# Batch 1's keys handed to the DMA queue nine steps ahead of their transposition, where it was four

## The chip, the cores and the metric

The kernel runs on one core of one Trainium2 chip. The metric is the device time of one execution in microseconds (us); lower is better. The engines are PE (TensorE, matrix products), DVE (VectorE), ACT (ScalarE), POOL (GpSimd) and SP (SyncE, which here does nothing but hand transfers to the DMA queue). Each engine works through its own list of instructions in order, and the lists meet only through semaphores.

## The reference, cut to what matters

```python
# q, k, v: (8, 8, 576, 64), p: (8, 8, 32, 64): batch, heads, sequence, width
p_packed = sm_attn(p, k, v)                  # 32 packed rows of each head attend to 576 keys
out = sm_attn(q, p_packed, p_packed)         # 576 queries of each head attend to the 32 packed rows
x = out.transpose(0, 2, 1, 3).reshape(4608, 512)
h = x @ w_in;  x = (h * cos(h)) @ w_out      # first layer, d_ff = 2048
h = x @ w2_in; y = (h * tanh(log1p(exp(h)))) @ w2_out   # second layer
```

The weights are float64 in memory and are turned into float32 on the chip: a load brings a chunk of 128 x 512 doubles (512 KB), ACT and DVE take its high and low words apart and put a float32 together.

## The kernel before, in words

The first layer runs over 4608 tokens in 16 tiles `t` of 288 tokens (two tiles for each batch) and over 16 chunks `s` of 128 hidden features. One pair (t, s) is one **step** n = 16 t + s. At step n PE forms the hidden block `h` in a PSUM bank of a ring of four (`l1`, lines 148 to 150), ACT and DVE make `h * cos(h)` of it (lines 913, 915, 916, 922, 928), and three steps later PE multiplies that with chunk s of `w_out` (`l2`; tile 0 uses line 953, later tiles lines 148 to 150). The last of these, line 928, reads the bank for the last time, so it also sets the bank free. Of tile 0 the chunks of `w_out` are used as plain float32; for the tiles after it ACT casts each to the fast format (line 630) and POOL forms the remainder (line 631).

Everything else is laid beside these steps by a table of step numbers: `at_ld(n, f)` records transfers at step n, `at_pe` and `at_ew` products and element-wise work. The numbers set the order in which the program is recorded; a scheduler then sets the final order on each engine. So one number in the table can move instructions on all five lists.

What stands beside the first steps:

- `w_load` (line 507 loads, lines 520 to 526 convert, 531 stores): the 16 chunks of `w_in`. `w_unit` (line 577) multiplies each with the packed rows of batch 0.
- `wo1_unit` (line 608 loads into one of two buffers `raw`; lines 620, 621 and 625 convert): the 16 chunks of `w_out`, called chunk 0 to 15 here. Chunk n is loaded at step n - 2 and converted at step n. A load can only start when the chunk two before it has been converted.
- `k_unit(b, g)`: the packed rows of batch b, heads 4 g to 4 g + 3. Its loads are eight transfers: four of `p` (line 234, 16 KB each, tile `pc`) and four of `k` (line 153, 272 KB each, tile `kr`, 32 partitions with four runs of 544 floats). DVE transposes both (lines 264 and 159), PE multiplies them (289), DVE takes the maxima (304 to 306), ACT the exponentials (312), PE transposes these (328, 329) and multiplies them with `v` (354; `v` is loaded at lines 244 and 249). There are two buffers `kr`, shared with `q_unit(t)`, which loads the queries of tile t (line 153, four transfers of 272 KB).

For batch 1 the table says `K1_OFF = (13, 18)`: the transposition of heads 0 to 3 is recorded at step 13, that of heads 4 to 7 at step 18, and their loads four steps ahead of it, at steps 9 and 14. The unit of batch 2's heads 0 to 3 and the queries of tile 2 have their loads at step 21.

SP issues transfers in the order of its list. It rotates through eight semaphores, so an issue can also wait for the landing of the transfer that used its semaphore eight transfers earlier.

Of the kernel before, what the change touches and what calls it, by code (L numbers as in the profile page):

```python
# [30 lines left out]
Q_LD = 2  # L31
W_LD = 2
K1_OFF = (13, 18)
K1_LD = 4
W01 = (28, 0.8)
WO_OFF = 0
WO_SPLIT = 13
# [52 lines left out]
def build(tc, q, k, v, p, w1i, w1o, w2i, w2o, out):  # L90
    nc = tc.nc
    ctx = ExitStack()
    with ctx:
# [668 lines left out]
        def after_w(f, lim=CH_LIM):  # L762
            def run():
                if last_w[0] is None or STEP[0] > lim:
                    return f()
                with tc.issue_after(last_w[0]):
                    f()

            return run
# [7 lines left out]
        def at_ld(n, f):  # L777
            bg_ld.setdefault(n, []).append(f)
# [8 lines left out]
        def place(stages, steps, off=0):  # L787
            for (pe, ew), n in zip(stages, steps):
                if off:
                    pe, ew = pe and hp(pe, off), ew and hp(ew, off)  # L790
                if pe is not None:
                    at_pe(n, pe)
                if ew is not None:
                    at_ew(n, ew)
# [11 lines left out]
        for g in range(2):  # L806
            wo = lambda sh: wo_tile(sh, F32)
            wa = lambda sh: wab_tile(0, sh, F32)
            loads, vl, stages = k_unit(0, g, wo)
# [4 lines left out]
        loads, stages = q_unit(0, wa)  # L814
# [19 lines left out]
            at_ew(n + WO_SPLIT, split)  # L834
        for g, off in enumerate(K1_OFF):
            loads, vl, stages = k_unit(1, g, ld_tile)
            at_ld(off - K1_LD, after_w(loads))
            for i in range(3):
                at_ld(off + V_LD + i, after_w(vl[i]))
            place(stages, [off + i for i in K1_SUB])  # L840
# [9 lines left out]
        for j, n in enumerate(U_AT):  # L850
            loads, steps = w2o_unit(j)
# [12 lines left out]
        for pair in range(3):  # L864
# [3 lines left out]
            for b, g, off in zip((b0, b0, b0 + 1, b0 + 1), (0, 1, 0, 1), offs):  # L868
                loads, vl, stages = k_unit(b, g, ld_tile)
# [12 lines left out]
        for t in range(1, NT):  # L882
            n = Q_N[t - 1]
            loads, stages = q_unit(t)
# [438 lines left out]
```

## Time and profile before

| | |
|---|---|
| time, median of 3 runs (lowest to highest) | 1549.7 us (1548.65 to 1550.8) |
| the profiled execution's own time | 1550.71 us |
| its span, first to last instruction | 1548.9 us |
| PE busy | 1479.0 us, 95% |
| DVE busy | 1103.8 us, 71% |
| ACT busy | 888.7 us, 57% |
| POOL busy | 623.8 us, 40% |

Times in the rows further down are microseconds from the start of the span. The page cuts the span into 40 equal slices of 38.7 us; its digits are tenths of busy time, so the stage in question (steps 0 to some 25) is slices 2 to 4. A timeline row gives the start, the time from the first to the last end of a merged group, the engine, the line, the operation, output and inputs, and in square brackets how long the engine sat idle before it and which instruction or transfer ended that.

### The profile page before, as it was taken

What the parts mean: (1) busy time and instruction counts of PE and PEld (TensorE: products, weight loads), DVE (VectorE), ACT (ScalarE), POOL (GpSimd) and SP (SyncE); (2) the same over time, 40 slices, a digit from 0 to 9 for tenths busy, and PEclk for the clock granted to TensorE, in tenths of its full rate; (3) what the DMA queues carried; (4) which work ended last, traced back from release to release, by engine and by line L of the source; (5) the groups of instructions that cost most, each with busy time, mean ns of one, the idle gap of its engine ahead of it and who ended that gap; (6) DMA issues with size and microseconds to landing.
All of it is one profiled execution on the core that took longest, in us unless ns stands there. A gap on an engine that the chain in (4) does not pass through costs nothing.

```text
span 1548.9 us, 28952 instructions
## 1 busy us (share of the span) xinstructions
PE 1479.0 (95%) x9922; PEld 1302.3 (84%) x9922; DVE 1103.8 (71%) x2080; ACT 888.7 (57%) x1834; POOL 623.8 (40%) x618
## 2 busy tenths in 40 slices
PE   7788999999999999999999999999999999999998
PEld 5568778899977999789999887888889898888997
DVE  4786667777677877687775778678668857766756
ACT  3576767667767767666765555334443534454443
POOL 0053333345543654536754666224421622352102
PEclk9899999999999999999999999999999999999999
DMA  7897576445648646623313757668868977876886
GB/s 270 263 259 187 170 184 164 129 111 171 176 132 217 176 139 171 194 89 91 105 51 113 250 212 251 190 201 242 263 214 231 310 216 218 243 213 217 232 263 201
DMA packets 247410, 299.20 MB, mean 193 GB/s; under 512 B 103648, under 2 KB 131040, under 8 KB 247264
## 3 DMA queue, kind: packets, MB, share of 16 engines
q1 hardware_dynamic: 244976, 296.21, 64.1%
q8 instruction: 79, 1.29, 0.4%
q10 hardware_dynamic: 2288, 1.15, 0.3%
q14 instruction: 67, 0.55, 0.1%
HBM read 240.65 MB, written 56.62 MB: 192 GB/s over the span
## 4 chain that ended last, share of the span: by engine, by line
PE 58%; DVE 8%; ACT 5%; DMA 3%; issue 3%; POOL 1%; SPq 1%; DVEq 0%; ACTq 0%; POOLq 0%
PE acc L149 10%; PE acc L150 10%; PE acc L148 10%; PE ps L148 9%; PE ps L149 9%; PE ps L150 9%; DVE r L916 2%; DVE r L915 1%; ACT r L922 1%; DVE r L928 1%; DMA raw<-in_moe_w_out_dram 1%; DVE wab L1020 1%; ACT L922 1%; DMA raw<-in_moe_w_in_dram 1%; PE ps L577 1%
## 5 line engine op out<-in xcount | busy, mean ns | idle before, releaser
L940 POOL TENSOR_TENSOR gh<-r,gh 128x288 fp32r<-128x288 f32 x240 | 199.6, 840 | 302.6 <-ACT gh L937 211.0
L1078 POOL TENSOR_TENSOR gh<-t,gh 128x512 fp32r<-128x512 f32 (+1 forms) x108 | 143.7, 1334 | 352.8 <-ACT gh L1077 343.1
L149 PE MATMUL acc<-gh,wo 128*128 128x288 f32 x960 | 282.5, 299 | 0.6 <-POOL gh L940 0.6
L150 PE MATMUL acc<-gh,wo 128*128 128x288 f32 x960 | 279.2, 297 | 0.0
L148 PE MATMUL acc<-gh,wo 128*128 128x288 f32 x960 | 261.9, 302 | 1.7 <-ACT gh L937 0.9
L149 PE MATMUL acc<-gh,T 128*128 128x512 f32 (+1 forms) x560 | 207.0, 371 | 2.1 <-DVE gh L1078 1.6
L148 PE MATMUL ps<-wab,ws 128*128 128x512 f32 (+1 forms) x560 | 206.0, 369 | 1.6 <-DMA ws<-wst 1.2
L149 PE MATMUL ps<-wab,ws 128*128 128x512 f32 (+1 forms) x560 | 206.4, 369 | 0.0
L150 PE MATMUL ps<-wab,ws 128*128 128x512 f32 (+1 forms) x560 | 205.3, 369 | 0.0
L150 PE MATMUL acc<-gh,T 128*128 128x512 f32 (+1 forms) x560 | 205.1, 369 | 0.0
L148 PE MATMUL ps<-aT,wab 128*128 128x288 f32 x512 | 163.7, 320 | 35.4 <-DVE r L928 21.3
L149 PEld LDWEIGHTS acc<-gh,wo 128*128 128x128 f32 x960 | 182.7, 190 | 6.9 <-issue 5.1
L1078 DVE TENSOR_TENSOR gh<-wo,gh 128x512 fp32r<-128x512 f32 (+1 forms) x160 | 128.0, 806 | 83.3 <-ACT gh L1077 82.8
L922 ACT ACTIVATE r<-r,halfpi 128x288 f32<-128x288 f32 x256 | 135.9, 535 | 88.2 <-DVE r L916 86.0
L148 PEld LDWEIGHTS acc<-gh,wo 128*128 128x128 f32 x960 | 172.5, 190 | 14.8 <-issue 6.1
L150 PEld LDWEIGHTS acc<-gh,wo 128*128 128x128 f32 x960 | 182.2, 190 | 2.1 <-issue 2.1
L148 PE MATMUL acc<-gh,T 128*128 128x512 f32 (+1 forms) x560 | 182.0, 369 | 1.0 <-DMA T<-tst 0.8
L928 DVE TENSOR_TENSOR r<-r,ps 128x288 f32<-128x288 f32 x240 | 107.3, 450 | 72.6 <-ACT r L922 72.3
L913 ACT ACTIVATE ki<-ps,quarter 128x288 int32<-128x288 f32 x256 | 124.6, 497 | 52.8 <-PE ps L150 41.2
L149 PE MATMUL ps<-aT,wab 128*128 128x288 f32 x512 | 154.0, 301 | 0.0
L150 PE MATMUL ps<-aT,wab 128*128 128x288 f32 x512 | 153.7, 300 | 0.0
L148 PEld LDWEIGHTS ps<-aT,wab 128*128 128x128 f32 x512 | 98.7, 193 | 62.2 <-DVE r L928 28.6
(193 smaller groups left out, 3061.7 us busy)
## 6 DMA issues: line engine op xcount, KB each, us to landing
T<-tst SPq DMA_DIRECT2D x280, 256.0 KB, 3.0
ws<-wst SPq DMA_DIRECT2D x224, 256.0 KB, 3.0
ld<-ws SPq DMA_DIRECT2D x80, 256.0 KB, 3.7
kr<-in_q_dram SPq DMA_DIRECT2D x60, 272.0 KB, 5.8
kr<-in_k_dram SPq DMA_DIRECT2D x56, 272.0 KB, 5.3
tst<-wt SPq DMA_DIRECT2D x56, 256.0 KB, 2.1
wst<-ws SPq DMA_DIRECT2D x56, 256.0 KB, 2.7
x2d<-xo SPq DMA_DIRECT2D x64, 144.0 KB, 1.7
```

Source lines behind the costliest of these rows:

```text
L148: nc.tensor.matmul(ps, l0, r0, start=first, stop=False, skip_group_check=more)
L149: nc.tensor.matmul(ps, l0, r1, start=False, stop=False, skip_group_check=more)
L150: nc.tensor.matmul(ps, l1, r0, start=False, stop=last, skip_group_check=more)
L577: return nc.tensor.matmul(st[b][32 * l : 32 * l + 32], PK[(b, g)][r : r + 64, 32 * l : 32 * l + 32], ms[h // 2]["m"][r : r + 64], start=Tr ...
L913: nc.scalar.activation(ki, st["h"], AF.Identity, bias=quarter, scale=1.0 / TWO_PI)
L915: nc.vector.scalar_tensor_tensor(r, ki, -TWO_PI, st["h"], ALU.mult, ALU.add)
L916: (nc.gpsimd if n % C_MOD in C_POOL else nc.vector).tensor_scalar(r, r, 1.570796, -4.712388, ALU.min, ALU.max)
L922: nc.scalar.activation(g, g, AF.Sin, bias=halfpi, scale=1.0)
L928: nc.vector.tensor_tensor(g, r, st["h"], ALU.mult)
L940: nc.gpsimd.tensor_tensor(gh[:, 1], st["g"], gh[:, 0], ALU.subtract)
L1020: (nc.gpsimd if k % 2 == 0 else nc.vector).tensor_tensor(x[:, a, 1, :n], src, x[:, a, 0, :n], ALU.subtract)
L1078: eng.tensor_tensor(hl[:, 1, :n], src, hl[:, 0, :n], ALU.subtract)
```

## The change

One constant becomes a pair, and its use picks an element of it. Both elements are 9, so the loads of batch 1's two key units are recorded at steps 4 and 9 in place of 9 and 14. The transpositions and all that follows them keep their steps.

```diff
-K1_LD = 4
+K1_LD = (9, 9)
...
         for g, off in enumerate(K1_OFF):
             loads, vl, stages = k_unit(1, g, ld_tile)
-            at_ld(off - K1_LD, after_w(loads))
+            at_ld(off - K1_LD[g], after_w(loads))
```

No instruction is added or taken away. What the scheduler makes of it is seen in the lists. The first place is SP's list from the load of chunk 12 on. In the names below `raw` is the buffer of a chunk of `w_out`, `kr` and `pc` hold keys (or queries) and `p`. Before, chunks 12 to 15 stand together, and the keys of batch 1's heads 4 to 7 (`kr_989`) come behind them:

```order
L531 DMA ws_813<-wab_669 128x512
L608 DMA raw_871<-in_moe_w_out_dram 128x1024
L608 DMA raw_898<-in_moe_w_out_dram 128x1024
L608 DMA raw_927<-in_moe_w_out_dram 128x1024
L608 DMA raw_959<-in_moe_w_out_dram 128x1024
L234 DMA pc_988<-in_p_dram 32x4x32
L153 DMA kr_989<-in_k_dram 32x4x544
L234 DMA pc_988<-in_p_dram 32x4x32
L153 DMA kr_989<-in_k_dram 32x4x544
```

Now the last part of that list reads as follows; `raw_937` is chunk 14, `raw_969` chunk 15, `kr_1301` batch 2's heads 0 to 3 and `kr_1310` the queries of tile 2:

```order
L234 DMA pc_1300<-in_p_dram 32x4x32
L153 DMA kr_1301<-in_k_dram 32x4x544
L234 DMA pc_1803<-in_p_dram 32x4x32 x2
L153 DMA kr_1310<-in_q_dram 32x4x544
L608 DMA raw_937<-in_moe_w_out_dram 128x1024
L153 DMA kr_1310<-in_q_dram 32x4x544 x3
L608 DMA raw_969<-in_moe_w_out_dram 128x1024
L244 DMA ld_1040<-in_v_dram 128x2x256
```

Three units (the four transfers each of batch 1's heads 4 to 7, of batch 2's heads 0 to 3 and of tile 2's queries) have moved from behind chunk 15 to ahead of it. Batch 1's heads 0 to 3 stood ahead of chunk 15 already; they have moved from behind chunk 11 to behind chunk 6, ahead of the last four chunks of `w_in`.

The second place is ACT's list from the conversion of chunk 15 (line 620) to the first `r` of tile 1 (`r_1058`, line 922; `ki_1056` is the first step of its chain, line 312 the exponentials of batch 1's heads 0 to 3). Before, chunk 15 stands thirteen rows ahead of the exponentials, and casts, cosines and the chain of tile 0 fill the distance:

```order
L620 ACTIVATE wab_919<-raw_959 128x512
L913 ACTIVATE ki_1023<-ps_998,quarter 128x288
L630 CAST wo_1061<-wo_485 128x512
L630 CAST wo_1097<-wo_486 128x512
L922 ACTIVATE r_977<-r_977,halfpi 128x288
L630 CAST wo_1151<-wo_486 128x512
L630 CAST wo_1207<-wo_487 128x512
L630 CAST wo_1253<-wo_487 128x512
L630 CAST wo_1292<-wo_488 128x512
L630 CAST wo_1351<-wo_488 128x512
L630 CAST wo_1413<-wo_489 128x512
L922 ACTIVATE r_1025<-r_1025,halfpi 128x288
```

Now it is followed by eight casts and the first instruction of two steps of tile 1:

```order
L620 ACTIVATE wab_929<-raw_969 128x512
L630 CAST wo_1061<-wo_485 128x512
L630 CAST wo_1097<-wo_486 128x512
L630 CAST wo_1151<-wo_486 128x512
L630 CAST wo_1207<-wo_487 128x512
L630 CAST wo_1253<-wo_487 128x512
L913 ACTIVATE ki_1056<-ps_1042,quarter 128x288
L630 CAST wo_1292<-wo_488 128x512
L630 CAST wo_1351<-wo_488 128x512
L630 CAST wo_1413<-wo_489 128x512
L913 ACTIVATE ki_1089<-ps_1069,quarter 128x288
L312 ACT_TABLE_LOAD
```

All cosines of tile 0 now stand ahead of chunk 15, and behind it come the casts, `ki` of tile 1's first two steps, a table load, the two exponentials, one more cast, a second table load and the cosine of `r_1058`.

The third place is DVE's list around the transposition of batch 2's heads 0 to 3 (lines 264 and 159, `pc_1300` and `kr_1301`). Now it stands between the maxima of batch 1's heads 0 to 3, with the conversion of chunk 15 (lines 621 and 625) in the middle:

```order
L304 TENSOR_REDUCE sm_1035<-ps_1006 128x1
L304 TENSOR_REDUCE sm_1035<-ps_1005 128x1
L264 STREAM_TRANSPOSE pp_1418<-pc_1300 128x128
L159 STREAM_TRANSPOSE kt_1420<-kr_1301 128x576 x2
L305 TENSOR_REDUCE sm_1035<-sm_1035 128x1
L621 TENSOR_SCALAR cvt_1031<-raw_969 128x512
L306 TENSOR_SCALAR sm_1035<-sm_1035 128x1
```

Before, all four maxima stood together, chunk 15 stood ahead of them, and the transposition came after them, between lines 915 and 916 of `r_1058`.

## Rows read from the trace of the kernel before

**Rows 1.** The page: span, each engine's share, and PE in 40 slices.
```profile
span 1548.9 us, 28952 instructions
PE 1479.0 (95%) x9922; PEld 1302.3 (84%) x9922; DVE 1103.8 (71%) x2080; ACT 888.7 (57%) x1834; POOL 623.8 (40%) x618
...
PE   7788999999999999999999999999999999999998
```
**Rows 2.** Timeline of PE: groups that waited, and three products between them.
```profile
85.27 1.06 PE L577 MATMUL ps<-wab,pk 64*32 64x512 f32 x8 [0.59 <-DVE g L928]
...
117.78 0.40 PE L148 MATMUL ps<-aT,wab 128*128 128x288 f32 x1 [3.74 <-DVE r L928]
...
118.69 0.56 PE L148 MATMUL acc<-gh,wo 128*128 128x288 f32 x3
120.32 0.44 PE L354 MATMUL ps<-ld,a 64*32 64x64 f32 x8 [1.07 <-ACT a L337]
```
**Rows 3.** PE waits from 0 to 300 us: who for whom, total, times, longest.
```profile
PE ps L577 <- DVE wab L526: 1.3, 1, 1.3
```
**Rows 4.** DVE waits from 70 to 150 us, the same columns.
```profile
DVE pp L264 <- DMA pc<-in_p_dram: 1.6, 1, 1.6
...
DVE kt L159 <- DMA kr<-in_k_dram: 0.2, 1, 0.2
```
**Rows 5.** Timeline of DVE ahead of the release at 117.32.
```profile
114.59 0.31 DVE L264 STREAM_TRANSPOSE pp<-pc 128x128 f32<-128x128 f32 x1 [1.63 <-DMA pc<-in_p_dram]
114.82 1.22 DVE L916 TENSOR_SCALAR r<-r 128x288 f32<-128x288 f32 x1
115.97 1.43 DVE L159 STREAM_TRANSPOSE kt<-kr 128x576 f32<-128x576 f32 x2
117.32 0.41 DVE L928 TENSOR_TENSOR r<-r,ps 128x288 f32<-128x288 f32 x1
```
**Rows 6.** Timeline of SP: issues from chunk 12 on; keys and queries behind chunk 15.
```profile
86.79 9.42 SPq L608 DMA_DIRECT2D raw<-in_moe_w_out_dram  x4
96.26 0.42 SPq L234 DMA_DIRECT2D pc<-in_p_dram  x1
...
104.37 0.33 SPq L234 DMA_DIRECT2D pc<-in_p_dram  x1
...
110.01 3.14 SPq L153 DMA_DIRECT2D kr<-in_q_dram  x4
```
**Rows 7.** Stretches: busy time of PE, PEld, DVE, ACT, POOL; clock; DMA share; GB/s.
```profile
82.00:92.00 10.00, 8.79 (x52) 6.06 (x53) 9.83 (x22) 6.75 (x12) 1.46 (x2) 1.00 1.04 295
92.00:98.00 6.00, 3.79 (x20) 2.78 (x19) 6.00 (x12) 5.01 (x10) 4.21 (x3) 1.00 0.49 129
98.00:104.00 6.00, 5.59 (x20) 4.56 (x21) 5.95 (x11) 4.88 (x11) 3.51 (x3) 0.72 1.09 256
104.00:120.00 16.00, 11.51 (x72) 8.77 (x70) 10.81 (x22) 11.75 (x24) 14.35 (x13) 0.98 1.08 243
...
130.00:140.00 10.00, 10.00 (x109) 9.53 (x108) 4.70 (x16) 7.71 (x15) 2.21 (x3) 1.00 0.69 183
140.00:150.00 10.00, 9.23 (x91) 7.86 (x89) 5.71 (x18) 6.55 (x13) 1.61 (x2) 1.00 0.46 128
```
**Rows 8.** DMA from 60 to 82 us, mostly weights: packets, volume, mean rate.
```profile
DMA packets 2582, 7.51 MB, mean 341 GB/s; under 512 B 287, under 2 KB 287, under 8 KB 2581
```
**Rows 9.** Timeline of ACT: chunk 15, casts, the exponentials, and what follows them.
```profile
100.13 0.66 ACT L620 ACTIVATE wab<-raw 128x512 f32<-128x512 f32 x1
...
102.54 3.21 ACT L630 CAST wo<-wo 128x512 fp32r<-128x512 f32 x6
...
109.00 1.28 ACT L312 ACT_TABLE_LOAD   x1 [1.28 <-DVE sm L306]
110.30 0.50 ACT L312 ACTIVATE tmp<-ps,sm 128x288 f32<-128x288 f32 x1
...
111.27 0.50 ACT L913 ACTIVATE ki<-ps,quarter 128x288 int32<-128x288 f32 x1
111.65 0.62 ACT L630 CAST wo<-wab 128x512 fp32r<-128x512 f32 x1
112.29 1.28 ACT L922 ACT_TABLE_LOAD   x1
116.08 0.54 ACT L922 ACTIVATE r<-r,halfpi 128x288 f32<-128x288 f32 x1 [2.51 <-DVE r L916]
...
118.10 0.40 ACT L966 COPY xo<-acc 128x288 f32<-128x288 f32 x1
118.39 0.59 ACT L336 COPY tmp<-ps 128x512 f32<-128x512 f32 x1
...
120.00 0.26 ACT L337 COPY a<-ps 64x128 f32<-64x128 f32 x1
```

## The prediction

> **What bounds the kernel now.** I read the page first, then the stretches of the stage that the change touches, then the timelines of PE, DVE, ACT and SP there. The page says that PE is busy 95% of a span of 1548.9 us and that only the first four of its 40 slices show 7 and 8 tenths [rows 1]. Past some 160 us PE is the bound almost without a gap, so whatever delay it has collected by then stays to the end, and whatever is saved there is kept. The change moves transfers between 60 and 125 us, so the question is when PE gets through that stretch.
>
> In it PE is not its own bound. From 82 to 98 us DVE is busy 9.83 of 10 and 6.00 of 6 us [rows 7]: it converts weights, and PE follows it. From 98 to 120 us the DMA engines are full (share 1.09 and 1.08) [rows 7]. The longest wait of PE in the stretch is one of 3.74 us that ends at 117.78, where a hidden block of tile 1 needs a free PSUM bank, and line 928 on DVE frees it; a second of 1.07 us ends at 120.32 and waits for ACT's copy at line 337 [rows 2]. Behind that PE is busy 10.00 of 10 us from 130 to 140 and 9.23 from 140 to 150 [rows 7]. So **117.78 and 120.32 are the clock by which I judge the change**: if the same two products start later, the kernel ends later by about as much.
>
> What stands ahead of 117.78 in the rows before: DVE waits 1.63 us for the `p` of batch 2's unit, needs 1.22 us for one line 916 and 1.43 us for two transpositions, and only then does line 928 at 117.32 [rows 5]. None of that is batch 1's keys. DVE waited for a key transfer once between 70 and 150 us, for 0.2 us [rows 4]. The change therefore brings early what was hardly waited for; its time comes from what it moves out of the way, or into it.
>
> **The change part by part.** (1) Batch 1's keys themselves. Their arrival saves at most the 0.2 us of [rows 4]; DVE is full there, so the next item is late instead. I take 0.
>
> (2) The first unit now stands ahead of the last four chunks of `w_in`. It is four transfers of 272 KB, 1.11 MB; the DMA engines move 341 GB/s from 60 to 82 us [rows 8] and are full afterwards at 82 to 92 [rows 7]. At the 243 GB/s of a stretch that is mostly keys and queries [rows 7] it costs 1.11 / 0.243 = 4.6 us. By so much the products of line 577 can come later; PE waited 1.3 us for their conversion once already [rows 3]. Whether that reaches 117.78 depends on DVE, which is the fuller engine until 98 us and has the same instructions to do in either order. I take 0, since the unit's bytes lie ahead of chunk 15 in both lists; the cover is DVE's backlog, and without it the cost is up to 4.6 us. That is the upper end.
>
> (3) Chunks 14 and 15 of `w_out` now stand behind the second key unit of batch 1, the first of batch 2 and the queries of tile 2. Before, all four chunks from 12 on were issued between 86.79 and 96.21 and those units followed at 96.26, 104.37 and 110.01 [rows 6]; ACT converted chunk 15 at 100.13 and did not wait for it [rows 9]. Now twelve transfers of 272 KB are queued ahead of it: 3.34 MB. At 243 GB/s that is 13.7 us. Some of it fills a hole: from 92 to 98 us the engines' share was 0.49 [rows 7] because SP stood waiting for a free `raw` buffer, and with keys to move that hole of 6 x 0.51 = 3.1 us closes. So chunk 15 arrives some 10.6 us later, at about 110.7 in place of 100.1. The bounds: 13.7 us without the credit, and 3.34 / 0.341 = 9.8 less 3.1 = 6.7 us if keys went at the rate of [rows 8]. I take the middle one because the 243 GB/s were measured on these very kinds of transfer, at full engines.
>
> (4) What hangs on chunk 15 on ACT. In the new list its conversion (line 620) is followed in order by five casts, a line 913, three casts, another 913, the table load, two exponentials, a cast, the second table load and the cosine of tile 1's first block, then line 928 on DVE. From [rows 9]: 0.6 + 5 x 0.535 (six took 3.21) = 3.3; 913 from 111.27 to 111.65 is 0.4, so 3.7; three casts 1.6, 5.3; 913 0.4, 5.7; table 1.3, 7.0; exponentials from 110.30 to 111.27 1.0, 8.0; cast 0.5, 8.5; table 1.3, 9.8; cosine 0.5, 10.3; line 928 0.4 [rows 5], **10.7 us**. The bank is free at 110.7 + 10.7 = 121.4. Before, the product started at 117.78: **3.6 us later**. DVE's line 306 for the exponentials stands behind chunk 15's line 621 as well, but the two are ready within a microsecond of the arrival and ACT gets to the exponentials 6 us after it, so DVE adds nothing.
>
> The second clock agrees. Line 337 follows the cosine through two copies of line 966, a cast, a second cosine, line 336 and itself: 0.3 + 0.5 + 0.3 + 0.45 + 0.5 + 0.3 = 2.3 [rows 9]. So 110.7 + 10.3 + 2.3 = 123.3 against 120.32, 3.0 later, and three products that lay before line 354 (0.56) [rows 2] now come behind it: 3.5.
>
> (5) What goes. DVE's wait of 1.63 us for batch 2's `p` goes, since that unit now lands ahead of chunk 15, and its transpositions come before the release and not just ahead of it. That would open the bank at 117.32 - 1.63 - 1.43 = 114.3 [rows 5] if ACT were ready. By (4) ACT is not: what is late next is chunk 15. I take 0, and up to 3.1 us plus the second wait of 1.07 [rows 2] is the lower end.
>
> (6) POOL forms the remainders behind ACT's casts and is busy 14.35 of 16 us from 104 to 120 [rows 7]. Its run moves later with the casts. What reads the remainders are the products of tile 1, all behind 117.78, and the casts ahead of the exponentials do not wait for POOL in the row of 102.54 [rows 9]. I take 0.
>
> The sum is 3.5 us. Against the profiled execution's own 1550.71 (span 1548.9 and 1.8 around it) that is 1554.2; the median of the runs is 1.0 below that execution, so 1549.7 + 3.5 = **1553.2 us**. Both are the same shift. A measurement of this kernel can tell some 0.2%, 3.1 us, from no change, so this is just beyond it.
>
> **A rule weighed.** In the rows a stretch of keys and queries moves 243 GB/s at a DMA share of 1.08, and one of weights 341 [rows 7, 8]. The Trainium skill, page "DMA: Bandwidth & Descriptors", section Specifications, gives 512 B as the smallest transfer that runs at line rate. A key run is 544 floats, 2,176 B, so by that rule keys should cost what weights cost, chunk 15 would come 6.7 us later, and the sum would be nothing. The trace disagrees at 243; the measurement decides, and the rule's case is the first rival below.
>
> **The rivals.** *Keys at the weights' rate (no change).* If the keys, spread among other transfers, run at 341 GB/s, chunk 15 lands at 100.1 + 6.7 = 106.8 and the bank opens at 117.5, 0.3 earlier than before: 1549.4. For it: the twelve transfers are now mixed with chunks and stores. Against it: the stretch of 104 to 120 us had up to eight transfers under way as well. Chance 0.20.
>
> *The change does not do what it says (no change).* SP may be held at the new place by its rotating semaphores or by the buffer, so that the keys leave hardly sooner, and chunks 14 and 15 follow as they did. Then the stage keeps its clock: 1549.7. For it: SP stood 9.42 us over four issues [rows 6], so it is often held. Against it: the list has an order, and what is behind a held issue is held too. Chance 0.12.
>
> *The release comes early (faster).* One mechanism: batch 2's `p` and keys are there when DVE reaches them, so the 1.63 us of waiting and the transpositions leave the place ahead of line 928, and ACT follows. It decides in favour if chunk 15 lands before 117.78 - 10.7 = 107.1, and is worth 3.1 us from a landing before 104.0. With the wait for line 337 gone too the gain is 3.1 + 1.07 = 4.2: 1545.5. For it: the 3.74 us of PE are the longest wait in the stretch, and the DMA had a hole. Against it: twelve transfers ahead of chunk 15. Chance 0.21.
>
> **How the numbers follow.** The forecast, slower by the queue ahead of chunk 15, has 0.47, with its own range 1550.5 (landing at 108) to 1558.0 (the 4.6 us of part 2 on top of 3.5, 1557.8). Of that 0.02 falls within 0.2%, so with the rivals' 0.20 and 0.12: faster 0.21, same 0.34, slower 0.45. The range reaches down to the faster rival, a little short of its full gain, and up past part 2 by 1.2 us for a PE that is throttled after a longer wait (from 98 to 104 us, behind a stretch in which PE was busy 3.79 of 6, the clock granted was 0.72, so in part at the lower of its two levels, 1.2 against 2.4 GHz) [rows 7]: 1546.0 to 1559.0.
>
> **What would show it.** Right: in the timeline of ACT after the change the line 620 of chunk 15 starts near 111, after a wait for a transfer of `in_moe_w_out`, and the product that waits for line 928 starts near 121. Part 3 is wrong if chunk 15 lands before 107; part 4 if ACT waits again between it and the exponentials; part 2 if the last products of line 577 (85.27 before [rows 2]) come over 4 us late and the delay is still there at 117. The forecast as a whole is wrong if PE starts that product before 117.8, or if PE, late there, catches up before 160 us.

## The result

The changed kernel takes 1562.07 us in the median of five runs (1559.39 to 1567.32), the kernel before 1549.70 (1544.88 to 1550.80): 12.4 us more by the medians. The recorded ratio is 1.0089, with a 95% interval of 1.0069 to 1.0110. The forecast was 1553.2, slower by 3.5, in a range up to 1559.0. The direction is right, the size is not, and the time lies outside the range.

The profiled execution is the slowest of the five (1567.32, span 1565.5). Its page says that the work is the same, and that the third and fourth of the 40 slices of PE went from 8 tenths to 7, and two later ones from 9 to 8, as against [rows 1]:

```profile
span 1565.5 us, 28952 instructions
...
PE 1482.1 (95%) x9922; PEld 1303.4 (83%) x9922; DVE 1104.2 (71%) x2080; ACT 887.7 (57%) x1834; POOL 621.2 (40%) x618
...
PE   7777999999999989998999999999999999999998
```

The stretches answer to [rows 7], in the same columns:

```profile
82.00:92.00 10.00, 6.05 (x31) 3.67 (x30) 8.23 (x19) 7.47 (x11) 2.36 (x2) 1.00 0.62 219
92.00:98.00 6.00, 5.79 (x36) 3.96 (x34) 5.33 (x11) 3.08 (x6) 1.53 (x2) 1.00 1.10 270
98.00:104.00 6.00, 4.18 (x24) 3.35 (x22) 5.20 (x11) 4.45 (x10) 1.60 (x2) 1.00 1.06 285
104.00:120.00 16.00, 11.94 (x60) 8.68 (x61) 9.12 (x21) 5.68 (x12) 3.97 (x4) 0.89 1.05 257
...
130.00:140.00 10.00, 9.08 (x105) 7.75 (x97) 7.22 (x19) 6.93 (x16) 7.68 (x8) 0.93 0.46 130
140.00:150.00 10.00, 8.67 (x98) 8.33 (x99) 3.75 (x10) 7.35 (x16) 2.37 (x3) 1.00 0.43 91
```

The hole of the DMA engines at 92 to 98 us (share 0.49 before) is filled. But 82 to 92, which had 1.04, now has 0.62: 10 x 0.38 = 3.8 us lost, where 3.1 were lost before. The hole has moved, and PE is down to 6.05 of 10 us in it (8.79 before). ACT and POOL, 11.75 and 14.35 of 16 us at 104 to 120 before, do 5.68 and 3.97: they wait for chunks.

The timeline of SP shows the moved list, where [rows 6] had chunks 12 to 15 in four issues from 86.79 on. The rows are those of chunks 11, 12 with 13, 14 and 15:

```profile
89.43 0.33 SPq L608 DMA_DIRECT2D raw<-in_moe_w_out_dram  x1
...
94.62 0.82 SPq L608 DMA_DIRECT2D raw<-in_moe_w_out_dram  x2
...
104.94 0.35 SPq L608 DMA_DIRECT2D raw<-in_moe_w_out_dram  x1
...
108.62 0.35 SPq L608 DMA_DIRECT2D raw<-in_moe_w_out_dram  x1
```

ACT's timeline answers to [rows 9], from the conversion of chunk 14 on:

```profile
112.56 0.68 ACT L620 ACTIVATE wab<-raw 128x512 f32<-128x512 f32 x1 [4.58 <-DMA raw<-in_moe_w_out_dram]
...
117.03 0.69 ACT L620 ACTIVATE wab<-raw 128x512 f32<-128x512 f32 x1 [3.28 <-DMA raw<-in_moe_w_out_dram]
117.62 2.68 ACT L630 CAST wo<-wo 128x512 fp32r<-128x512 f32 x5
...
120.61 1.64 ACT L630 CAST wo<-wo 128x512 fp32r<-128x512 f32 x3
...
122.66 1.28 ACT L312 ACT_TABLE_LOAD   x1
123.95 0.50 ACT L312 ACTIVATE tmp<-ps,sm 128x288 f32<-128x288 f32 x1
```

ACT waits 4.58 and 3.28 us for the last two chunks, and the exponentials start at 123.95 in place of 110.30. DVE's timeline, for [rows 5], and its waits from 70 to 150 us, for [rows 4]:

```profile
98.43 0.31 DVE L264 STREAM_TRANSPOSE pp<-pc 128x128 f32<-128x128 f32 x1 [1.01 <-DMA pc<-in_p_dram]
...
127.41 0.45 DVE L928 TENSOR_TENSOR r<-r,ps 128x288 f32<-128x288 f32 x1 [1.18 <-ACT r L922]
```

```profile
DVE cvt L621 <- DMA raw<-in_moe_w_out_dram: 4.8, 2, 4.1
...
DVE pp L264 <- DMA pc<-in_p_dram: 1.8, 2, 1.0
```

The 1.63 us for batch 2's `p` are gone, but the waits for `p` sum to 1.8 us as they did to 1.6, and 4.8 us for chunks have come on top. PE, for [rows 2]:

```profile
92.57 1.06 PE L577 MATMUL ps<-wab,pk 64*32 64x512 f32 x8
...
127.92 0.61 PE L148 MATMUL ps<-aT,wab 128*128 128x288 f32 x1 [1.50 <-DVE r L928]
...
129.73 0.44 PE L354 MATMUL ps<-ld,a 64*32 64x64 f32 x8
```

The last products of line 577 come 7.3 us later (85.27 before), the first clock, the product at 127.92, 10.1 later (117.78 before), and the second, line 354, 9.4 later (120.32 before). Set beside each other, the executions of line 928 in the two traces lie 3.4 us apart at 85 us, 10.9 at 160 to 200 and 12.7 at the end of the first layer. This one execution loses up to 4 us more in the second layer; the other four are up to 8 us shorter, and what it loses there was not traced further.

### The profile page after: what moved, and what is told of

Same layout as the page of the kernel before. It is cut to its first block, busy times and chain, and to the rows that moved or that the text cites. A ratio compares the mean times of both kernels' runs of the same rounds, so it can differ in the third digit from the quotient of the medians.

```text
span 1565.5 us, 28952 instructions
## 1 busy us (share of the span) xinstructions
PE 1482.1 (95%) x9922; PEld 1303.4 (83%) x9922; DVE 1104.2 (71%) x2080; ACT 887.7 (57%) x1834; POOL 621.2 (40%) x618
## 4 chain that ended last, share of the span: by engine, by line
PE 53%; DVE 6%; issue 6%; ACT 5%; DMA 4%; POOL 4%; SPq 1%; DVEq 0%; ACTq 0%; POOLq 0%
PE acc L149 10%; PE acc L150 10%; PE acc L148 10%; PE ps L148 8%; PE ps L150 7%; PE ps L149 7%; POOL ws L671 2%; DVE r L916 1%; DMA ws<-wst 1%; ACT r L922 1%; DVE r L915 1%; DMA T<-tst 1%; DVE r L928 1%; DVE wab L1020 1%; PE ps L577 1%
```

## The experiments

`K1_LD` holds how many steps ahead the two units of batch 1 are loaded: (9, 9) in the changed kernel, (4, 4) in the one before. `CH_LIM` is the step from which a load is held behind the last weight chunk. Diffs are against the changed kernel, e17's against the one before. All times in the table are of the profiled execution of each. At 66 us the executions already stand up to 2.5 us from the kernel before, so only larger differences in a column mean something. The last column is the recorded ratio to the runs of the kernel before; microseconds in the text are differences of medians, and the two need not agree exactly (e7: 1.7 us by the medians, 1.0001 by the ratio).

| kernel | chunk 15, L620 | first exponential, L312 | first L354 | ratio (95%) |
|---|---|---|---|---|
| before | 100.13 | 110.30 | 120.32 | 1 |
| changed (9, 9) | 117.03 | 123.95 | 129.73 | 1.0089 (1.0069 to 1.0110) |
| e1 (9, 4) | 104.36 | 120.13 | 127.44 | 1.0081 (1.0061 to 1.0102) |
| e2 (4, 9) | 115.54 | 118.04 | 126.93 | 1.0032 (1.0016 to 1.0048) |
| e3 (9, 9), limit 24 | 109.51 | 116.94 | 128.19 | 1.0042 (1.0028 to 1.0057) |
| e4 (9, 9), casts free | 116.41 | 124.63 | 131.93 | 1.0083 (1.0064 to 1.0101) |
| e5 (4, 9), limit 24 | 107.03 | 113.69 | 118.71 | 1.0041 (1.0026 to 1.0056) |
| e6 (7, 4) | 102.11 | 121.96 | 129.26 | 1.0089 (1.0069 to 1.0109) |
| e7 (4, 7), limit 24 | 101.30 | 108.75 | 117.88 | 1.0001 (0.9990 to 1.0012) |
| e8 (3, 4) | 103.06 | 112.95 | 120.40 | 0.9993 (0.9978 to 1.0007) |
| e9 (9, 9), casts two steps later | 117.19 | 119.69 | 129.44 | 1.0054 (1.0035 to 1.0073) |
| e10 (14, 4) | 103.79 | 115.20 | 124.04 | 1.0032 (1.0018 to 1.0046) |
| e11 (14, 7), limit 24 | 104.33 | 117.98 | 124.64 | 1.0032 (1.0017 to 1.0047) |
| e12 (9, 4), transpositions held | 105.81 | 123.44 | 131.77 | 1.0084 (1.0065 to 1.0103) |
| e13 (14, 4), transpositions held | 99.86 | 112.42 | 119.83 | 0.9984 (0.9968 to 1.0000) |
| e14 (9, 9), transpositions held | 117.84 | 123.98 | 129.78 | 1.0062 (1.0041 to 1.0082) |
| e15 (14, 7), limit 24, held | 100.88 | 119.76 | 127.19 | 1.0053 (1.0037 to 1.0069) |
| e16 (9, 4), casts behind EXP | 104.78 | 114.48 | 123.57 | 1.0041 (1.0024 to 1.0058) |
| e17 (4, 4), casts behind EXP | 103.57 | 113.80 | 122.19 | 1.0016 (1.0004 to 1.0028) |
| e18 e13, casts behind EXP | 102.02 | 112.02 | 120.88 | 1.0002 (0.9990 to 1.0013) |

How much of a loss is there when PE leaves the stage can be counted in the traces. Take PE's products of lines 148 to 150 in order and compare their starts with those of the kernel before. Between 165 and 200 us the changed kernel is 10.9 us behind, e1 10.9, e2 6.9, e3 7.6, e5 0.1, e9 10.4, e12 15.8, e15 7.2, e16 6.4 and e17 4.4; e7 is 2.2 and e13 1.4 ahead. Where this and the ratio part, the loss arises behind the stage.

### Which of the moved loads costs it

```
-K1_LD = (9, 9)
+K1_LD = (9, 4)      # e1: the first unit alone
+K1_LD = (4, 9)      # e2: the second unit alone
-CH_LIM = 20         # e3, e5: batch 2's unit and tile 2's queries
+CH_LIM = 24         #         go back behind chunk 15
```

> Only the first key unit (batch 1, heads 0 to 3) is loaded nine steps ahead; the second is loaded four steps ahead as in the kernel before. Four key transfers (1.09 MB) so pass the last four w_in chunks, and no more data stands ahead of w_out's chunk 15 than in the kernel before. Theory T (the delay is the data queued ahead of chunk 15, some 4.5 us a unit at 243 GB/s, passed on through ScalarE's list): chunk 15 converted between 99 and 104 us (100.1 before, 117.0 in the changed kernel), the product behind the second clock's bank between 117 and 120 us, total +0 to +3 us. Rival R1 (the first unit ahead of the w_in chunks does most of it, by way of VectorE's list of conversions): chunk 15 after 108 us, total +6 to +10 us. Rival R2 (ScalarE's order of casts, pinned behind chunk 15): the order here is that of before, total +0.

> Only the second key unit (batch 1, heads 4 to 7) is loaded nine steps ahead; the first stays four steps ahead. Three units (batch 1 heads 4 to 7, batch 2 heads 0 to 3, query tile 2) then stand ahead of chunk 15 that stood behind it, and ScalarE's list behind chunk 15 is shorter than in the changed kernel (four casts and no cast ahead of the exponentials but one, against eight). Theory T: chunk 15 converted at 111 to 114 us (13.7 us of transfers, with or without 3 us of queue time that stood empty before), the bank's product 6 to 8 us behind it at 118 to 122 us, total +1 to +5 us. R1: 0 to +1 us, chunk 15 at 101 to 104. R2: by the shorter list, total 0 to +1 us wherever chunk 15 lands.

> The changed kernel with batch 2's first key unit and query tile 2 held behind chunk 15 again, as they were in the kernel before; both of batch 1's units stay nine steps ahead. Theory T: one unit more than before stands ahead of chunks 12 to 15, and part of the first unit's detour: chunk 12 as in the changed kernel (100 us), chunk 15 at 105 to 109 us, not 117; ScalarE's list behind it is as long as in the changed kernel, so the bank's product is 10 to 11 us later, 116 to 120 us (127.9 in the changed kernel); total 0 to +3 us. R1 (the first unit does it): total +6 us or more. R2 (the list of casts behind chunk 15, which is longer still here): total +6 us or more.

> The second key unit (batch 1, heads 4 to 7) is loaded nine steps ahead, the first stays at four, and batch 2's first unit and query tile 2 are held behind chunk 15: one unit (1.09 MB), not three, stands ahead of chunks 12 to 15 that stood behind them before. Theory T2 (each unit put ahead of a weight chunk in this stretch delays it by about 4.5 us, and the conversions behind it pass that on through the in-order lists of VectorE and ScalarE): chunk 15 converted at 103 to 106 us (100.1 before), the first unit's exponentials at 113 to 116 us (110.3 before), total +3 to +5 us. Rival S (the delay is made by batch 2's unit and the query tile, which have no slack to use; one unit fits into the 3 us in which the queue stood empty at 92 to 98 us): exponentials within 1 us of before, total -1 to +1 us.

The first unit, which the prediction took at nothing, costs 13.2 us by the medians when it is moved alone, as much as the whole change and more than any of the expectations allowed (e1). The second move costs 6.6 (e2); with two of the three units back behind chunk 15, both units of batch 1 cost 7.6 (e3), and the second of them alone 6.7 (e5). The parts don't add up: 13.2 and 6.6 are more than 12.4, and e3, which moves both units, costs less than e1, which moves one. They delay the same exponentials, and every version has its own lists.

Nor does chunk 15 rank the kernels. In e2 it lands at 115.54, in e1 at 104.36, and e1 is the slower one. So the argument "chunk 15 sets the release" holds for the changed kernel only. ACT's timeline of e1 shows what stands in its place:

```profile
104.36 0.67 ACT L620 ACTIVATE wab<-raw 128x512 f32<-128x512 f32 x1
104.94 4.24 ACT L630 CAST wo<-wo 128x512 fp32r<-128x512 f32 x8
109.08 1.52 ACT L922 ACTIVATE r<-r,halfpi 128x288 f32<-128x288 f32 x3
...
118.83 1.28 ACT L312 ACT_TABLE_LOAD   x1 [5.79 <-DVE sm L306]
```

The scores of line 289 on PE, in the kernel before and in e1, and DVE's timeline of e1:

```profile
105.15 0.72 PE L289 MATMUL ps<-kt,pp 64*32 64x288 f32 x16
```

```profile
111.96 1.21 PE L289 MATMUL ps<-kt,pp 64*32 64x288 f32 x16 [3.34 <-DVE g L928]
```

```profile
106.98 1.76 DVE L625 SCALAR_TENSOR_TENSOR wab<-wab,cvt 128x512 int32<-128x512 int32 x1
108.66 1.37 DVE L916 TENSOR_SCALAR r<-r 128x288 f32<-128x288 f32 x1
109.95 0.30 DVE L264 STREAM_TRANSPOSE pp<-pc 128x128 f32<-128x128 f32 x1
110.18 1.39 DVE L159 STREAM_TRANSPOSE kt<-kr 128x576 f32<-128x576 f32 x2
111.50 1.14 DVE L928 TENSOR_TENSOR g<-r,ps 128x288 f32<-128x288 f32 x3
113.27 0.82 DVE L304 TENSOR_REDUCE sm<-ps 128x1 f32<-128x288 f32 x2 [0.63 <-PE ps L289]
118.22 0.31 DVE L264 STREAM_TRANSPOSE pp<-pc 128x128 f32<-128x128 f32 x1 [4.13 <-DMA pc<-in_p_dram]
...
118.60 0.15 DVE L306 TENSOR_SCALAR sm<-sm 128x1 f32<-128x1 f32 x1
```

Two things delay the exponentials here. The first is the scores: they wait 3.34 us for line 928, which frees their bank, and start at 111.96 (105.15 before). On ACT a block of eight casts stands ahead of three cosines that line 928 needs. But DVE isn't seen waiting for a cosine: its timeline has no gap from 96.18 to 112.64, and between the first of these cosines (done at 109.6) and line 928 its own list has a line 916 and the transposition of batch 1's second unit. How much the casts add is therefore not read from a wait. They add in another way too: they release the remainders on POOL (line 631, nine in a row from 105.61 to 117.31), and beside them lines 625 and 916 take 1.76 and 1.37 us, where e16 has 0.68 and 0.30.

The second comes on top. The maxima are done at 114.09 (108.55 before), but DVE's list has batch 2's `p` ahead of lines 305 and 306, and DVE waits 4.13 us for it. ACT waits 5.79 us for line 306. In the kernel before, this transposition comes behind line 306.

### The hole: filled, or moved

```
-K1_LD = (9, 9)      # e7: the second unit exactly between
+K1_LD = (4, 7)      #     chunks 13 and 14
-CH_LIM = 20
+CH_LIM = 24
```

> The second key unit is loaded seven steps ahead and everything behind it is held behind chunk 15: it stands between chunks 13 and 14, where in the kernel before the queue waits some 7 us for the two raw buffers to come free (its four chunk loads take 9.42 us to hand over, the transfers' share falls to 0.49 at 92 to 98 us). The first unit stays at four. Theory T2 with the hole (transfers that stand where the queue is held anyway cost only what is longer than the hole, 4.5 less 3.1 us): chunk 15 at 100 to 103 us, exponentials at 109 to 112 us, total -2 to +2 us, and batch 2's first unit arrives about 3 us earlier than in the kernel before, so that VectorE's wait of 1.63 us for it is gone. Rival D (any unit ahead of a chunk costs its 4.5 us): chunk 15 at 104 to 106 us, total +3 to +5 us.

e5 and e7 move the same four transfers: in e5 they stand ahead of chunk 12, in e7 between 13 and 14. By the medians the one costs 6.7 us and the other 1.7, by the ratios 1.0041 and 1.0001; e7's interval includes no change. The stretches of e5, then of e7, columns as in [rows 7]:

```profile
92.00:98.00 6.00, 4.94 (x25) 3.96 (x26) 3.65 (x10) 2.62 (x6) 0.67 (x1) 1.00 1.01 260
98.00:104.00 6.00, 2.83 (x10) 1.95 (x9) 6.00 (x13) 3.32 (x7) 2.70 (x2) 0.82 0.45 105
```

```profile
92.00:98.00 6.00, 3.89 (x21) 3.12 (x22) 6.00 (x13) 4.05 (x9) 2.71 (x3) 1.00 1.09 230
98.00:104.00 6.00, 6.00 (x40) 4.21 (x39) 5.93 (x11) 4.82 (x10) 2.86 (x3) 1.00 1.10 331
```

In e5 the hole is as large as before (share 0.45) and stands six microseconds later. Its cause is that chunk 14 goes into the `raw` buffer of chunk 12 and SP waits until DVE and ACT have converted that; SP's timeline of e5 has the same held group as [rows 6], only later:

```profile
91.13 11.16 SPq L608 DMA_DIRECT2D raw<-in_moe_w_out_dram  x4
```

What stands ahead of chunk 12 delays chunk 12, its conversion, and so the hole. What stands right at the wait fills it, as in e7. In this stage the difference is worth 2.3 us (e5 0.1 behind the kernel before at 165 to 200 us, e7 2.2 ahead; at 66 us they stood 0.9 apart). The rest of e5's loss arises behind 250 us: its products are still only 0.3 us late there and 3.9 at the end of the first layer. So the 6.7 us are not the price of the hole.

### The first unit, step by step

```
+K1_LD = (7, 4)      # e6: ahead of fewer chunks
+K1_LD = (3, 4)      # e8: one step later than before
+K1_LD = (14, 4)     # e10: issued at 19 to 30 us, ahead of the last eight w_in chunks
+K1_LD = (14, 7)     # e11, with CH_LIM = 24: e10 and e7 together
```

> The first key unit is loaded seven steps ahead in place of four, the second at four: it passes w_out's chunks 9 to 11 and the last two w_in chunks, but not the two w_in chunks and w_out's chunks 7 and 8 that it passes at nine. Theory T2 (a unit of transfers ahead of a w_in chunk, in a stretch in which the queue never stands empty, delays that chunk's conversion and all behind it, whether VectorE has a backlog or not): the last w_in chunk's product 3 to 6 us later than 85.3 us, total +4 to +8 us. Rival B (VectorE's backlog covers it, as the prediction had it, and the loss in the first-unit-only kernel came from the two chunks at 60 to 72 us, where VectorE waits for data): the product within 1.5 us of before, total -1 to +2 us.

> The other direction: the first key unit is loaded three steps ahead in place of four, between chunk 12 and chunk 13. Theory T2: chunk 12 was not waiting for the unit but for a raw buffer, so it gains little, and the unit arrives 2 to 4 us later than before, with VectorE waiting for it ahead of its transpositions (91.1 us before, with 0.17 us of wait): total +1 to +4 us. Rival E (earlier is only worse, later is better all along): total -1 to -4 us.

> The first key unit is loaded fourteen steps ahead, the second four. The first unit is so handed over at about 18 us, behind the first two w_out chunks, and its transfers fall into the stretch from 28 to 46 us, where the transfers' share is 0.24, 0.45 and 0.22; VectorE's transpositions of it come at 30 and 67 us, when it has no backlog. No w_in or w_out chunk stands behind it that could have been transferred in that time. Theory T2 (what counts is what a unit displaces, not how early it is): no delay of the w_in chunks (products at 82.6 and 85.3 us as before), the unit's 4.5 us of transfers gone from 79 to 92 us and 1.7 us of transpositions gone from VectorE's backlog there, total -5 to 0 us. Rival H (earliness itself costs: the unit holds one of the two key buffers 40 us longer, and the query tile's loads behind it wait for the other): total +2 to +8 us.

> The first key unit fourteen steps ahead, in the stretch where the queue stands empty (28 to 46 us), and the second between chunks 13 and 14 as in the run with the second unit ahead of chunk 14, the rest held behind chunk 15. Theory T2: both units are out of the way of every chunk: chunk 15 at 98 to 102 us, exponentials at 105 to 111 us (110.3 before), total -6 to 0 us, at or a little below the run with the first unit alone in the empty stretch. Rival H (earliness itself costs): +2 to +8 us.

Ahead of fewer chunks the unit costs no less (e6, +15.2 by the medians, where 8 was the most expected); a step later than before it costs nothing (e8). In the emptier queue ahead of 46 us (share 0.25 from 30 to 46 us before) it costs 4.5 (e10), though its bytes should be out of the way there; with e7's move on top it is 5.3 (e11). DVE's and PE's timelines of e10 say why:

```profile
69.10 2.10 DVE L159 STREAM_TRANSPOSE kt<-kr 128x576 f32<-128x576 f32 x3 [0.49 <-DMA raw<-in_moe_w_out_dram]
...
71.69 0.77 DVE L159 STREAM_TRANSPOSE kt<-kr 128x576 f32<-128x576 f32 x1
```

```profile
90.22 1.06 PE L577 MATMUL ps<-wab,pk 64*32 64x512 f32 x8 [0.63 <-DVE g L928]
```

With keys there early, the order of DVE's work changes too: its two transpositions come at 69 to 72 us, next to two of the queries, which the kernel before has at 67.38; they are now ahead of conversions of `w_in`, and the last products of line 577 start at 90.22 in place of 85.27.

### DVE's list

The transpositions of batch 1's first unit are put back behind the conversion of chunk 11; in e12, e13, e14 and e15 with the loads of e1, e10, the changed kernel and e11.

```
 def s0():
-    nc.vector.transpose(pp, ...); st["pp"] = pp; trans(0)
+    with behind(("c", 11) if (b, g) == (1, 0) else None):
+        nc.vector.transpose(pp, ...); st["pp"] = pp; trans(0)
...
-    nc.vector.tensor_scalar(t, st["r"][:, :, 0], 29, ...)
+    marks[("c", ft)] = nc.vector.tensor_scalar(t, st["r"][:, :, 0], 29, ...)
```

> The kernel with only the first unit nine steps ahead, and the unit's transpositions on VectorE held behind the start of chunk 11's conversion, their place in the kernel before. Loads in the order of the first-unit-only kernel (+13.2 us). Theory L (the list: transpositions brought forward, with their waits for the keys, stand ahead of the w_in and w_out conversions): last w_in chunk's product within 2 us of 85.3, total 0 to +5 us. Theory X (the transfers: the chunks come late whatever VectorE's order): last w_in product at 90 to 93 us as without the hold, total +8 to +13 us.

> The first unit loaded in the empty stretch of the queue (fourteen steps ahead) with its transpositions held behind the start of chunk 11's conversion. Against the same loads without the hold (+4.5 us). Theory L: the last w_in product back at 85 to 87 us and the unit's transfers out of the way of chunks 12 to 15, total -3 to +1 us. Theory X (something in the early loads themselves, such as w_in's stores or the key buffer that is held): +3 to +6 us as without the hold.

> The changed kernel (both units nine steps ahead) with the first unit's transpositions held behind the start of chunk 11's conversion. Theory L: the first unit's share goes and the three units ahead of chunk 15 stay, as in the kernel with the second unit alone nine steps ahead (+6.6 us): total +5 to +9 us. Theory X: total +11 to +14 us as in the changed kernel.

> The first unit in the empty stretch with its transpositions held behind the start of chunk 11's conversion, the second unit between chunks 13 and 14, the rest held behind chunk 15. Theory L: total -4 to +1 us, against +5.0 without the hold. Theory X: +3 to +6 us.

In the emptier queue it was DVE's list: e10's +4.5 us becomes -2.9 (e13), and PE's timeline of e13 has the products nearly where they were:

```profile
86.72 1.06 PE L577 MATMUL ps<-wab,pk 64*32 64x512 f32 x8
```

In e1's place it was not: e12 costs 12.6 us where e1 cost 13.2, and its last products of line 577 start at 94.82, no earlier than e1's at 92.69. In the changed kernel it is some 2 of 12.4, if anything (e14, +10.4, the intervals overlap). e15 puts two moves together that cost nothing each, and should have cost nothing; it costs 8.4, though chunk 15 lands at 100.88. ACT's timeline of e15 has the block of eight casts again, and no cosine until 105.60:

```profile
100.88 0.68 ACT L620 ACTIVATE wab<-raw 128x512 f32<-128x512 f32 x1
101.45 4.26 ACT L630 CAST wo<-wo 128x512 fp32r<-128x512 f32 x8
105.60 0.55 ACT L922 ACTIVATE r<-r,halfpi 128x288 f32<-128x288 f32 x1
```

The block alone is not the cost: e13, which loses nothing, has the same eight casts behind chunk 15 (4.24 us from 100.43 on), but two cosines stand ahead of chunk 15 there (0.97 us from 99.00 on), and its scores start at 107.00 against 114.43 in e15.

### ACT's list behind chunk 15

Casts are held behind the latest conversion of a chunk (line 629). e4 takes that away (and all queries of tile 2 are loaded ahead of chunk 14 there); e9 puts the casts two steps later in the plan, with the loads in the same order; e16 places what is planned after the exponentials of tile 1's first unit behind them, with the loads of e1, and e17 and e18 do so in the kernel before and in e13.

```
 # e4
-    with tc.issue_after(getattr(wm_last[0], "ins", wm_last[0])):
+    if True:
 # e9
-WO_SPLIT = 13
+WO_SPLIT = 15
 # e16 to e18
-    wm_last[0] = nc.scalar.activation(WM[ft], ...)
+    marks[("wm",)] = nc.scalar.activation(WM[ft], ...)
...
-    with tc.issue_after(getattr(wm_last[0], "ins", wm_last[0])):
+    with behind(("act", 0, 1, 0) if ("act", 0, 1, 0) in marks else ("wm",)):
```

> The changed kernel without the order that holds the casts of w_out behind the last conversion, so that ScalarE takes most casts ahead of chunk 15 and two behind it before the exponentials; the loads keep the changed kernel's places but for query tile 2, all of it now ahead of chunk 14. Theory T: chunk 15 is converted as late as in the changed kernel (115 to 119 us), but ScalarE's list behind it takes some 6 us in place of 10.4, so that the bank's product starts near 123 us (127.9 in the changed kernel): total +4 to +8 us against the kernel before, 4 to 6 us less than the changed kernel. R2 (the list is all of it): total within 2 us of the kernel before. If the list were not in the path at all (the transfers of keys bind by themselves): no change against the changed kernel, +12 us.

> The changed kernel with its loads in the same order, but the casts of w_out's chunks placed two steps later: behind chunk 15 ScalarE then has one cast ahead of the first unit's exponentials and their table load, not eight casts and two other conversions, and the scheduler puts VectorE's scale for the exponentials ahead of chunk 15's conversion. Theory T2 (chunk 15 comes late by its queue, and ScalarE's list passes it on): chunk 15 at 115 to 118 us as in the changed kernel (117.0), the exponentials at 118 to 121 us (123.95), the product that waits for the bank at 122 to 124 us (127.9), total +7 to +9 us against the kernel before, 4 to 5 us less than the changed kernel. Rival V (VectorE's lateness alone makes the delay, and ScalarE's list lies beside it): +11 to +13 us, as the changed kernel. Rival R2 (the list is all of it): 0 to +2 us.

> The kernel with only the first unit nine steps ahead, loads in the same order, but the casts of w_out traced after the first unit's exponentials are placed behind these on ScalarE: one cast then stands between chunk 15's conversion and the exponentials in place of ten or eleven. Theory A (ScalarE's list enlarges the delay): chunk 15 at 103 to 106 us as without the edit (104.4), the exponentials at 109 to 115 us (120.1), total +4 to +9 us against the kernel before (+13.2 without the edit). Theory X (the chunks' arrival is all of it): exponentials within 2 us of 120, total +11 to +14 us.

> Control: the kernel before, loads untouched, with the casts of w_out placed behind the first unit's exponentials on ScalarE. Theory A, where the casts are in the path in the kernel before too: exponentials at 106 to 110 us (110.3), total -5 to 0 us. If they aren't in its path: within 1 us, or slower by up to 4 us, where the products of the second layer's first steps then wait for the casts.

> The first unit loaded in the empty stretch of the queue, its transpositions held behind the start of chunk 11's conversion (-2.9 us), and the casts of w_out behind the first unit's exponentials. Theory A: chunk 15 at about 100 us, exponentials at 106 to 110 us (112.4 without the casts' move), total -7 to -2 us. If the casts aren't in the path there: -4 to +1 us.

e9 leaves chunk 15 where it is (117.19) and takes casts from behind it: the exponentials start at 119.69 in place of 123.95, and 8.6 us of loss are left of 12.4. The stage shows little of that gain: the first line 354 comes at 129.44 (129.73 in the changed kernel), since the eight casts now stand ahead of the second cosine of tile 1, whose line 928 waits 3.77 us, and at 165 to 200 us PE is 10.4 us behind against 10.9. Where the rest of the gain arises was not traced. e4 does not help (+13.5, where 4 to 8 were expected): free casts gather in other places of ACT's list, and the exponentials stay at 124.63.

e16 is the test of e1's chain. One cast is left ahead of the table load, and the scores of line 289 no longer wait:

```profile
104.78 0.69 ACT L620 ACTIVATE wab<-raw 128x512 f32<-128x512 f32 x1
105.35 0.62 ACT L630 CAST wo<-wo 128x512 fp32r<-128x512 f32 x1
...
113.19 1.28 ACT L312 ACT_TABLE_LOAD   x1 [4.31 <-DVE sm L306]
```

```profile
108.80 0.71 PE L289 MATMUL ps<-kt,pp 64*32 64x288 f32 x16
```

But DVE's list has changed as well. Batch 2's `p` is now behind line 306:

```profile
112.93 0.15 DVE L306 TENSOR_SCALAR sm<-sm 128x1 f32<-128x1 f32 x1
...
118.49 0.31 DVE L264 STREAM_TRANSPOSE pp<-pc 128x128 f32<-128x128 f32 x1 [2.35 <-DMA pc<-in_p_dram]
```

The loss falls from 13.2 to 7.1 us, and the exponentials come 5.65 us earlier. Of these 1.4 are there when the maxima of line 304 are done (112.71 against 114.09); the other 4.3 are the transposition's place. So the larger part of what e16 gains on ACT is DVE's order and not the casts, and no run moves one without the other. e3 fits: the first unit stands where it does in e1, nine casts stand behind chunk 15 (4.76 us from 110.09 on), the transposition comes behind line 306 (117.51 and 114.16), and the loss is 7.6.

The same edit by itself costs 2.3 us in the kernel before (e17, 1552.15). With this list of casts the first unit's place is worth 1556.90 - 1552.15 = 4.75 us; the two medians have intervals of some 2 us each way, and in the stage it is 2.0 (6.4 against 4.4 us behind). That it is near the 4.6 that the prediction named for its transfer may be chance. In e13 the edit takes the gain away (e18, 1.0002 after 0.9984, where 2 to 7 us less than before were expected if the casts were in the path). No version beats the kernel before beyond doubt: e13 comes nearest, at 0.9984 (0.9968 to 1.0000).

## Why the prediction was wrong in size

**Part 2 failed: the first unit was taken at nothing.** The cover named was DVE's backlog, which has "the same instructions to do in either order". Its own sign came out: the products of line 577 are 7.3 us late, and the delay is still there at 117. Moved alone, the unit costs 13.2 us (e1). Some 4.75 of it is the unit's place in the queue with the lists of e16 and e17; that this is its transfer, paid by all that stands behind it, is argued from the size. Most of the rest goes with e16's edit (e1 against e16), which moves the casts and, with them, batch 2's `p` on DVE: by the traces the larger share is the 4.13 us that DVE waits for this `p` ahead of line 306, the smaller the late scores. The first unit's own transpositions, which now come earlier on DVE, are not the cause (e12). The error of reasoning: DVE had the same work, but not at the same time, since weight chunks that land later leave it 8.23 of 10 us busy at 82 to 92 (8.24 in e1) where it had 9.83. A backlog covers nothing if what is late is its own input.

**Part 3 was right in mechanism and 6.3 us short.** Chunk 15 was forecast at 110.7 and is converted at 117.03, after a wait of 3.28 us for its transfer. The term that failed is the credit of 3.1 us for the hole. e5 and e7 show it: ahead of the wait the hole moves, at the wait it fills. e2 tests the term without the first unit: chunk 15 comes 15.4 us late (115.54), where the forecast had 10.6 with the credit and 13.7 without; 1.7 us stay open. The first unit adds only 1.5 to that in the changed kernel (16.9), though alone it delays chunk 15 by 4.2 (e1). The price of 243 GB/s for keys and queries held well enough: the stretch of 104 to 120 us moves 257.

**Part 4 was right.** From chunk 15 to line 928 it gave 10.3 us, and it is 127.41 - 117.03 = 10.4, through the casts, table load and exponentials that the prediction listed. e9 shortens that list and has the exponentials 4.3 us earlier, but what it takes away there comes back at the next cosine.

**Part 5 was right as an order of events.** The wait for batch 2's `p` went and nothing came of it, since chunk 15 was later. **Part 1** stays without a price of its own. **Part 6** asked only whether anything waits for POOL; in e1 the remainders cost time beside DVE's lines 625 and 916 without any wait, some 2 us there. In the changed kernel POOL is busy only 3.97 of 16 us from 104 to 120.

**The premise that a delay is kept** behind 160 us holds for the changed kernel (10.9 us become 12.7 by the end of the first layer), but only to some 5 us: e9 goes from 10.4 to 4.9, e5 from 0.1 to 3.9.

**The two clocks were one too few.** Lines 928 and 354 carried the forecast as far as chunk 15 set them. In e1 and e15 chunk 15 is within a few microseconds of its old place, and the exponentials are 10 us late all the same: their input, line 306, was thought to be ready, "within a microsecond of the arrival".

**The rivals.** Keys at the weights' rate: refuted, chunk 15 is later than even the forecast has it. In the traces a packet of keys or queries, 2,176 B, takes 159 ns on average (kernel before, 104 to 120 us) and 164 in the changed kernel, not much less than a packet of weights of 4,096 B (185, kernel before, 60 to 82 us): 219 and 354 GB/s over 16 engines. The short packets of `p`, 128 B, are 6% of the engines' time in the first of these stretches, so they are not what makes it slow. The Trainium skill, page "DMA: Bandwidth & Descriptors", section Specifications, gives 512 B as the smallest transfer at line rate. These packets are above that size and do not reach the rate. The change does not do what it says: refuted by SP's timeline, in which the keys stand ahead of chunks 12 to 15. The release comes early: its condition, chunk 15 before 107.1, was not met; and e1 and e15 meet it and are slower too, so the condition was not enough.

**Open.** The casts and the place of batch 2's `p` were never moved one without the other, so their shares in e1 are read from traces only. All four cosines of e15 stand behind the casts, two of e13's ahead of them; e15 was not tried with the casts moved. e4's miss is read from its trace only. e5's loss behind 250 us and e9's gain behind the stage were not followed. The 12.4 us are not split into terms that add up: the two units meet in the same exponentials.

## What to carry to other kernels

A load that is issued earlier in an in-order queue delays everything it passes, unless the queue was idle there; and idle time that comes from a wait for a buffer moved along with what was put ahead of the wait, and was filled by what stood right at it. A moved load also changes the order of other engines' work, so read what each engine's list now puts between the late item and the next step of the chain: here a transposition that waited for its data, and casts, cost more than the unit's place in the queue (6.1 us against 4.75). And where an estimate rests on "this engine is full anyway", ask whether what it works on still arrives in time.

## What the runs showed of the hardware

- With keys, queries and `v` under way, the DMA engines of the changed kernel were full and slow: shares of 1.05 to 1.10 at 257 to 285 GB/s from 92 to 120 us, against 341 in [rows 8]. Chunk 15, one of the weights, took 117.03 - 108.62 = 8.4 us from issue to conversion in that company; in the kernel before it had landed 3.8 us after its issue.
- DVE's line 916 took 0.26 to 0.31 us wherever no POOL instruction ran beside it, and up to 1.38 where one did (60 to 160 us of the kernel before, the changed kernel, e1 and e16); line 625 took 0.67 to 0.69 and up to 1.76. Lines 928 and 915 took 0.39 to 0.46 either way. Why these two and not the others is not shown.
